# Moving one eighth of the output projection into the MLP pass, and splitting two sets of weights at other times, in a hand-scheduled attention + gMLP block

## The chip, the core and the metric

The kernel runs on one core of a Trainium2 chip. The metric is device time in microseconds (us) of the whole program, the median of several runs. Names used below: PE is TensorE (matmuls), ACT ScalarE, DVE VectorE, POOL GpSimd, SP the queue that issues most of the DMAs.

## The reference

One token block, S = 2048, D = 512, 32 heads of 16, F/2 = 896, all in float32:

```python
xn = layernorm(x)
q, k, v = heads(xn @ wqkv)                      # 32 heads of 16
o = softmax(q @ k.T * 16 ** -0.5) @ v
z = gelu(xn @ w_in)                             # 2048 x 1792
z1, z2 = z[:, :896], layernorm(z[:, 896:])
g = w_sp @ z2 + b_sp                            # 2048 x 2048 times 2048 x 896
out = x + heads_back(o) @ wo + (z1 * g) @ w_out
```

## The kernel before

**Precision.** A float32 operand is split into a rounded part and a remainder, [.., 0, ..] and [.., 1, ..] of one tile, and a product is three matmuls (high times high, low times high, high times low). The split of a weight tile is two POOL operations behind one load (`weight`, lines L286 and L288 for the function's two operations).

**Dense work.** All of the large projections go through `dense`: each *slot* is two matmuls that lie side by side in the upper and the lower 64 rows of the array, into the one PSUM tile `dps`. A *pass* (the two halves of `dps` filled and then read out) is 24 slots of z1 or z2, 96 of the spatial product, 42 of `mlp_out`, 24 of `attn_out`; the next pass can begin when `dps` has been copied out (`dfree`).

**Attention.** For each of 16 pairs of heads and 4 column groups, 16 key tiles: a score product *S* (then the exponential, on ACT, tile `pf`), a product *M* of the next pair whose row maximum DVE takes (tile `mm`, 128x1024), and in blocks of 8 key tiles a *value block V* of 32 matmuls (`sl<-pf,vall`). S, M and V share three PSUM tiles `sl`.

**The order.** A planner in the kernel walks through simulated time and writes the instructions of all engines in that order. Between two value blocks it goes through one line of `ORDER`, a string of S, M, D (one dense slot) and V. There are 128 value blocks, the last without M work behind it. The stretch behind block n is called *turn n* here, and turns 2k and 2k+1 together, from the start of block 2k to the start of block 2k+2, *pair k*: k runs from 1 to 63, and behind pair 63 stands block 128 and what is left. When no dense slot can be issued and nothing else either, PE gets a *filler* slot: two matmuls of zeros into `dps` (`filler`, `dps<-brow,zeror`). A slot list yields `"q"` at its ends: if more than 11 slots have gone into the turn, dense work holds until the next value block.

**Sequence of the dense work**, one generator after the other: `v_rest`, `qk_rest` (q and k of the other heads), `z2_all` (16 passes), `z1_all` (14 passes, gelu on POOL and ACT), `spatial` (w_sp times z2, 4 column groups of 512, each with 16 weight tiles `wsp`), `mlp_out` (7 blocks of `wout` against `hp`, the product z1 * g; the sum with x goes to a scratch), `attn_out` (4 blocks of `wo` against `op`, the normalised heads; the sum goes into `fin`, and `last_pair`, `last_mm`, `last_add` add the last pair of heads and store the result).

**Buffers.** Weights, z, and intermediate tiles live in one ring of 19 buffers (`piece`), counted by `room["big"]`; tasks start when `room` allows. `ahead_of_time` splits a weight tile early and writes both parts to a scratch in memory, from which `fetch_parts` reads them back; before the change the seven z1 weight tiles are handled so, right at the start. `norm_out(g4, c)` normalises eight heads of one column group (DVE, four POOL operations on `ob` and `ohl`, five DMAs) and writes them to `oscr`. It begins when its heads are done and the one buffer `ogrp` is free.

Of the kernel before, what the change touches and what calls it, by code (L numbers as in the profile page):

```python
# [16 lines left out]
P = 128  # L17
# [20 lines left out]
LEAD = 30  # L38
XAT = 8.0
# [17 lines left out]
def fused_block(ctx, tc, x, wqkv, wo, w_in, w_spT, b_sp, w_out, out):  # L57
# [56 lines left out]
    mscr = [dr.tile([4, 32, 32], F32, name=f"mscr{i}") for i in range(4)]  # L114
    w1scr = [dr.tile([P, 2, 512], F32, name=f"w1scr{f}") for f in range(NF)]
# [186 lines left out]
    def fetch_parts(out, k, scr, spare):  # L302
        yield "C", lambda: room["big"] > 1 + spare[0]
        t = piece(f"wf{k}")
        move(t, scr)
        yield "T", LOAD
        out[k] = t
# [314 lines left out]
    def z1_all():  # L622
        for g in range(NG):
# [52 lines left out]

    def load_b(g):
# [3 lines left out]
    def spatial():  # L681
        for n, (g, (x, y)) in enumerate(units):
            lone, opens, closes = x == y, x <= y, x >= y
            if n == 0:
                yield from need(lambda: room["t5"] > 3)
            if opens:
                for f in {x, y}:
                    load_z1(g, f)
# [11 lines left out]
            for s in range(NT):  # L700
# [14 lines left out]
                if s == 7:  # L715
                    yield "q",
            if lone:
# [49 lines left out]
    def mlp_load(t, q):  # L767
        hp = []
        for i, n in enumerate((4, 3)):
            h = piece(f"hp{t}_{q}_{i}")  # L770
            v = h[:, :, :n * P].rearrange("p a (f q) -> p a f q", q=P)
            for r, u in zip(HALVES, (t + q, t + 1 - q)):
                move(v[r], hscr[u // 4][r, :, u % 4, 4 * i:4 * i + n, :])
            hp.append(h)
        hps.append(hp)

    def mlp_out():
# [13 lines left out]
        for t in range(0, NT, 2):  # L791
            xt = load_x(t)
            if t == NT - 4:
                selectors()
                prepare(wo_, [(g, f"wo{g}", wo[g * P:(g + 1) * P, :], 512) for g in range(4)], spare=(-9,))
            for q in range(2):
# [7 lines left out]
                for f in range(NF):  # L804
# [3 lines left out]
                    yield from dense(1, ops, ops, (q, 1 - q), not q and f == 0, q == 1 and f == NF - 1)  # L808
# [4 lines left out]
        lease("big", NF)  # L813
# [49 lines left out]
    def norm_out(g4, c):  # L863
# [3 lines left out]
        yield open_("ogrp")  # L867
# [45 lines left out]
    def ao_load(t):  # L913
        ops = []
        for q in range(2):
            op = piece(f"op{t}_{q}").rearrange("p a (g q) -> p a g q", q=P)
            for r, u in zip(HALVES, (t + q, t + 1 - q)):
                for a in range(2):
                    move(op[r, a, 0:3, :], oscr[r, a, :, u * P:(u + 1) * P])
# [6 lines left out]
    def attn_out():  # L926
        def out_(t):
            yield "D", 1.22
# [4 lines left out]
        yield from need(lambda: len(wo_) == 4)  # L933
        for t in range(0, NT, 2):
# [5 lines left out]
            for q in range(2):  # L940
# [8 lines left out]
                yield from dense(4, lambda g: ops(g, False), lambda g: ops(g, True), (q, 1 - q), not q, q == 1)  # L949
# [54 lines left out]
    with tc.manual_schedule(engines=engines):  # L1004
# [325 lines left out]
```

## Time and profile before

| | |
|---|---|
| median of 3 runs | 1876.55 us (1875.42 to 1880.77) |
| the profiled execution | 1873.65 us, span 1871.9 us |
| granted PE clock | 0.994 |
| PE busy | 1821.7 us of matmuls, 1103.6 us of weight loads |
| DVE, ACT, POOL busy | 1443.5, 1188.7, 721.0 us |
| DMA | 297.75 MB, mean 159 GB/s |

Busy time of PE is a sum of windows that overlap in the pipeline, so 97% does not say that no matmul more would fit. What is of use here is the length of a pair (some 26 to 31 us) beside what stands in it.

### The profile page before, as it was taken

What the parts mean: (1) busy time and instruction counts of PE and PEld (TensorE: products, weight loads), DVE (VectorE), ACT (ScalarE), POOL (GpSimd) and SP (SyncE); (2) the same over time, 40 slices, a digit from 0 to 9 for tenths busy, and PEclk for the clock granted to TensorE, in tenths of its full rate; (3) what the DMA queues carried; (4) which work ended last, traced back from release to release, by engine and by line L of the source; (5) the groups of instructions that cost most, each with busy time, mean ns of one, the idle gap of its engine ahead of it and who ended that gap; (6) DMA issues with size and microseconds to landing.
All of it is one profiled execution on the core that took longest, in us unless ns stands there. A gap on an engine that the chain in (4) does not pass through costs nothing.

```text
span 1871.9 us, 38101 instructions
## 1 busy us (share of the span) xinstructions
PE 1821.7 (97%) x14848; PEld 1103.6 (59%) x14848; DVE 1443.5 (77%) x1677; ACT 1188.7 (64%) x1292; POOL 721.0 (39%) x808
## 2 busy tenths in 40 slices
PE   6989999999999999999999999999999999999998
PEld 5756566655654565466666656565655656555555
DVE  6568878888897887878787878777877878788863
ACT  2147777687676677766666666566656666666653
POOL 5412242778879768710145203400352222002110
PEclk9999999999999999999999999999999999999999
DMA  7836572533566343366568665744766757475544
GB/s 230 295 121 190 193 238 87 126 91 109 135 225 192 117 125 98 88 152 150 153 196 194 175 170 164 177 129 128 186 189 163 185 155 181 119 150 158 154 132 142
DMA packets 209309, 297.75 MB, mean 159 GB/s; under 512 B 36049, under 2 KB 107281, under 8 KB 206241
## 3 DMA queue, kind: packets, MB, share of 16 engines
q1 hardware_dynamic: 200008, 265.44, 51.8%
q0 software_dynamic: 9120, 29.89, 4.9%
q8 instruction: 116, 1.90, 0.4%
q14 instruction: 65, 0.52, 0.1%
HBM read 189.60 MB, written 105.65 MB: 158 GB/s over the span
## 4 chain that ended last, share of the span: by engine, by line
PE 85%; DVE 5%; POOL 4%; issue 2%; DMA 2%; ACT 1%; SPq 0%; DVEq 0%; POOLq 0%; ACTq 0%
PE dps L1181 33%; PE sl L1219 23%; PE sl L1122 14%; PE sl L1136 12%; DVE mm L839 4%; PE dps L1195 1%; POOL wsp L288 1%; ACT pf L74 1%; POOL wsp L286 1%; DMA zs<-z2scr 0%; PE sl L242 0%; PE sl L241 0%; PE sl L240 0%; POOL z2hl L542 0%; DMA kscr<-qkhl 0%
## 5 line engine op out<-in xcount | busy, mean ns | idle before, releaser
L839 DVE TENSOR_REDUCE mm<-sl 128x2 f32<-128x1024 f32 x1024 | 1224.2, 1222 | 209.2 <-PE sl L1136 204.7
L74 ACT ACTIVATE pf<-sl 128x1024 f32<-128x1024 f32 x1024 | 1041.1, 1026 | 337.3 <-PE sl L1122 300.1
L1219 PE MATMUL sl<-pf,vall 128*32 128x512 f32 x4096 | 467.3, 597 | 0.0
L1122 PE MATMUL sl<-qst,kst 50*128 50x512 f32 x2048 | 443.3, 422 | 14.0 <-DVE mm L839 5.1
L1181 PE MATMUL dps<-wsp,zs 64*128 64x512 f32 x2688 | 439.4, 393 | 2.7 <-DMA zs<-z2scr 2.7
L1136 PE MATMUL sl<-kst,qst 48*128 48x512 f32 x2048 | 427.1, 407 | 3.4 <-DVE mm L839 1.8
L1122 PEld LDWEIGHTS sl<-qst,kst 50*128 50x128 f32 x2048 | 197.7, 184 | 225.5 <-issue 84.0
L1181 PEld LDWEIGHTS dps<-wsp,zs 64*128 64x128 f32 x2688 | 265.0, 187 | 44.8 <-DMA zs<-z2scr 4.7
L1219 PEld LDWEIGHTS sl<-pf,vall 128*32 128x32 f32 x4096 | 120.3, 110 | 268.3 <-issue 236.1
L1136 PEld LDWEIGHTS sl<-kst,qst 48*128 48x128 f32 x2048 | 198.1, 185 | 109.6 <-ACT pf L74 57.6
L747 POOL TENSOR_TENSOR hhl<-z1i,hhl 128x512 fp32r<-128x512 f32 x28 | 35.6, 1284 | 371.4 <-ACT hhl L74 371.4
L74 ACT ACTIVATE e<-sl 128x512 f32<-128x512 f32 x64 | 38.2, 598 | 212.6 <-PE sl L1219 194.2
L1239 DVE TENSOR_TENSOR e<-sl,e 128x512 f32<-128x512 f32 x64 | 44.3, 692 | 132.3 <-PE sl L1219 68.9
L1181 PE MATMUL dps<-w,xt 64*128 64x448 f32 x768 | 110.8, 368 | 1.5
L1181 PE MATMUL dps<-wout,hp 64*128 64x512 f32 x672 | 109.6, 392 | 0.0
L882 POOL TENSOR_TENSOR ob<-ob 128x512 f32<-128x512 f32 (+1 forms) x16 | 20.5, 1282 | 193.6 <-DMA ob<-escr 193.6
L1181 PEld LDWEIGHTS dps<-w,xt 64*128 64x128 f32 x768 | 73.7, 186 | 16.1 <-issue 7.8
L438 POOL TENSOR_TENSOR qkhl<-qr,qkhl 128x512 fp32r<-128x512 f32 x24 | 30.4, 1283 | 129.5 <-ACT qkhl L74 93.3
L886 POOL TENSOR_TENSOR ob<-ob 128x512 f32<-128x512 f32 (+1 forms) x16 | 20.5, 1283 | 147.1 <-DMA ob<-rscr 147.1
L1181 PEld LDWEIGHTS dps<-wout,hp 64*128 64x128 f32 x672 | 65.2, 187 | 9.4
L1195 PE MATMUL dps<-brow,zeror 64*128 64x512 f32 x276 | 51.8, 399 | 0.5 <-DVE fin L929 0.3
L1181 PE MATMUL dps<-xnT,wqk 64*128 64x512 f32 x288 | 47.4, 396 | 1.1 <-ACT vall L74 0.4
(285 smaller groups left out, 1617.9 us busy)
## 6 DMA issues: line engine op xcount, KB each, us to landing
zs<-z2scr SPq DMA_DIRECT2D x192, 256.0 KB
escr<-e SPq DMA_DIRECT2D x60, 256.0 KB
hscr<-hhl POOLq DMA_DIRECT2D x28, 512.0 KB, 6.0
qst<-qscr SPq DMA_DIRECT2D x30, 384.0 KB
kst<-kscr SPq DMA_DIRECT2D x30, 384.0 KB
qscr<-qkhl SPq DMA_DIRECT2D x16, 512.0 KB
kscr<-qkhl SPq DMA_DIRECT2D x16, 512.0 KB
xscr<-xnT POOLq DMA_DIRECT2D x16, 512.0 KB, 6.7
```

The costliest lines, as they stand in the source:

```text
L74: return nc.scalar.activation(out, in_, func, **kw)
L438: nc.gpsimd.tensor_sub(hl[:, 1, :], raw_, hl[:, 0, :].bitcast(F32))
L747: nc.gpsimd.tensor_sub(hl[:, 1, :], z1, hl[:, 0, :].bitcast(F32))
L839: nc.vector.tensor_reduce(mmax[g][:, :, t, kc], sl[k], AX.X, ALU.max)
L882: nc.gpsimd.tensor_add(both_[rows, 0, :], both_[rows, 0, :], both_[rows, 1, :])
L886: nc.gpsimd.tensor_mul(both_[rows, 0, :], both_[rows, 0, :], both_[rows, 1, :])
L1122: nc.tensor.matmul(sl[k][:, j, :], kst[p % 2][rows, kt * P:(kt + 1) * P], qst[p % 2][rows, c * 512:(c + 1) * 512], start=True, stop=True)
L1136: nc.tensor.matmul(sl[k][:, j, :], qst[p % 2][rows, tt * P:(tt + 1) * P], kst[p % 2][rows, kc * 512:(kc + 1) * 512], start=True, stop=True)
L1181: nc.tensor.matmul(dps[:, bank, :w], lhs, rhs, start=go, stop=stop)
L1195: nc.tensor.matmul(dps[:, bank, :], zeror[r:r + 64], brow[r:r + 64], start=not begun, stop=not begun)
L1219: nc.tensor.matmul(sl[k][cols:cols + VW, 0, :], vpack(kt + r, 2 * p + j), pf[:, j * 512:(j + 1) * 512], start=n == n_pv, stop=n == n_pv + ...
L1239: nc.vector.tensor_add(e, sl[k][:, 0, :], e)
```

## The change

It has five parts:

- **An eighth block in `mlp_out`.** The rows of `wo` for heads 0 to 7 (`wo0`) are prepared with `wout`, and each pass of `mlp_out` takes an eighth block, the normalised first eight heads, loaded from `oscr` into the free quarter of the `hp` tile. `attn_out` takes 3 blocks in place of 4, so a pass of `mlp_out` has 48 slots in place of 42, and one of `attn_out` 18 in place of 24. Its read-out on DVE is issued only while a value block runs or after the last.
- **z1 weights later.** The `ahead_of_time` tasks of the seven z1 weight tiles are spawned at the start of `qk_rest`, not before the first scores.
- **Spatial weights earlier.** Eight of the 16 weight tiles of the first column group are split during `qk_rest` and written to a new scratch `wsscr`; they are fetched when z1 ends, and the other eight are split then.
- **`norm_out` of heads 0 to 7 waits** until eight quarters of the spatial product's input have been used (`OUTS`).
- The first `xnT` tiles of z1, and the first z1 tiles of the spatial product, are loaded by tasks of their own, and `z1_all` waits for the former, `spatial`'s read-out for the latter.

```diff
+KEPT = 8
+OUTS = 8
...
+    wsscr = [dr.tile([P, 2, 512], F32, name=f"wsscr{s}") for s in range(KEPT)]
...
     def qk_rest():
+        for f in range(NF):
+            owed[0] += 1
+            spawn(ahead_of_time(f, (f"w1_{f}", w_in[:, f * P:(f + 1) * P], D, ND), w1scr[f], AHEAD), 1)
         for g in (2, 3, 0, 1):
...
+                if (g, m) in ((3, 1), (0, 1)):
+                    for s in range(KEPT // 2) if g else range(KEPT // 2, KEPT):
+                        owed[0] += 1
+                        spawn(ahead_of_time(s, sp_weights(0, s), wsscr[s], AHEAD), 1)
...
+    fetched = [False]
+
+    def fetch_first():
+        for c in range(ND):
+            yield "C", lambda: room["big"] > 2
+            xnT[0, c] = piece(f"xnT0_{c}_")
+            move(xnT[0, c], xscr[0][c])
+        fetched[0] = True
+        late1[0] = 1
...
             if t == NT - 1:
-                yield from need(lambda: room["big"] > 5)
-                fetch_xnT(0)
-                late1[0] = 1
+                spawn(fetch_first(), 1)
...
     def z1_all():
+        yield from need(lambda: fetched[0])
...
-                    prepare(wsp, [((0, s), *sp_weights(0, s)) for s in range(NT)], spare=kept)
+                    for s in range(KEPT):
+                        spawn(fetch_parts(wsp, (0, s), wsscr[s], kept), 1)
+                    prepare(wsp, [((0, s), *sp_weights(0, s)) for s in range(KEPT, NT)], spare=kept)
...
-                    prepare(wout, [(f, f"wout{f}", w_out[f * P:(f + 1) * P, :], 512) for f in range(NF)], spare=(2,))
+                    prepare(wout, [(f, f"wout{f}", w_out[f * P:(f + 1) * P, :], 512) for f in range(NF)] + [(NF, "wo0", wo[0:P, :], 512)], spare=(2,))
...
             for r, u in zip(HALVES, (t + q, t + 1 - q)):
                 move(v[r], hscr[u // 4][r, :, u % 4, 4 * i:4 * i + n, :])
+                if i:
+                    move(h[r, :, n * P:], oscr[r, :, 0, u * P:(u + 1) * P])
...
-                for f in range(NF):
+                for f in range(NF + 1):
...
-        yield open_("ogrp")
+        yield "C", lambda: room["ogrp"] > 0 and (g4 or zused[0] > OUTS)
...
         def out_(t):
+            yield "C", lambda: mode == "V" or n_pv == N
             yield "D", 1.22
             nc.vector.tensor_add(fin[t], dps, fin[t])
...
-                yield from dense(4, lambda g: ops(g, False), lambda g: ops(g, True), (q, 1 - q), not q, q == 1)
+                yield from dense(3, lambda g: ops(g + 1, False), lambda g: ops(g + 1, True), (q, 1 - q), not q, q == 1)
...
-        for f in range(NF):
-            owed[0] += 1
-            spawn(ahead_of_time(f, (f"w1_{f}", w_in[:, f * P:(f + 1) * P], D, ND), w1scr[f], AHEAD), 1)
```

Where the instructions land shows in the order of the two programs. On SP, at the write of the first maxima (`mscr<-ms`) and their read back into the rows of q (`qst<-mscr`), on which the first scores wait, there stood before the loads of the z1 weights (`w_2r` to `w_5r`) and the writes of their parts (`w1scr`):

```order
L129 DMA w_2r<-in_w_in 128x4x128
L129 DMA w1scr_167<-w_0_885 128x1024
L129 DMA w1scr_168<-w_1_886 128x1024
L129 DMA w_3r<-in_w_in 128x4x128
L129 DMA w1scr_169<-w_2_908 128x1024
L129 DMA w_4r<-in_w_in 128x4x128
L129 DMA w_5r<-in_w_in 128x4x128
L129 DMA mscr_163<-ms_980 128x32
L129 DMA qst_90<-mscr_163 2x16x32 x2
```

and now:

```order
L132 DMA wqk_1r<-in_wqkv 128x4x128
L132 DMA mscr_163<-ms_966 128x32
L132 DMA qst_90<-mscr_163 2x16x32 x2
L132 DMA mscr_164<-ms_1167 128x32
L132 DMA qst_90<-mscr_164 2x16x32 x2
L132 DMA w_0r<-in_w_in 128x4x128
L132 DMA w_1r<-in_w_in 128x4x128
```

The seven loads and seven writes of the z1 weights now stand behind the first two of these round trips. On PE, in the first turn behind the last pass of z1, there stood before, between the S (`qst,kst`) and M (`kst,qst`) products, filler slots alone:

```order
L1122 MATMUL sl_195<-qst_91,kst_93 128x512 x2
L1136 MATMUL sl_193<-kst_92,qst_90 128x512 x2
L1195 MATMUL dps<-brow,zeror 128x512 x2
L1122 MATMUL sl_194<-qst_91,kst_93 128x512 x2
L1195 MATMUL dps<-brow,zeror 128x512 x4
L1136 MATMUL sl_195<-kst_92,qst_90 128x512 x2
```

and now, two turns earlier in the program, the spatial product with the fetched tiles (`wf`) against its input (`zs`):

```order
L1149 MATMUL sl_203<-qst_91,kst_93 128x512 x2
L1163 MATMUL sl_202<-kst_92,qst_90 128x512 x2
L1208 MATMUL dps<-brow,onesr 128x512 x2
L1208 MATMUL dps<-wf_0_7821,zs_7818 128x512 x6
L1149 MATMUL sl_201<-qst_91,kst_93 128x512 x2
L1208 MATMUL dps<-wf_0_7823,zs_7818 128x512 x2
```

The turns of zeros behind z1 are gone, and what follows stands earlier. At the end, on PE behind the last value block, where `on` and `e` belong to the last pair of heads, there stood before two passes of `attn_out` (this is the first half of them):

```order
L977 MATMUL sl_194<-sel,on_19811 128x512 x2
L977 MATMUL sl_195<-sel,on_19811 128x512 x2
L962 MATMUL sl_193<-e_3_19810,sel 32x128 x8
L1181 MATMUL dps<-wo_18600,op_0_19821 128x512 x6
L1181 MATMUL dps<-wo_18612,op_0_19821 128x512 x6
L1181 MATMUL dps<-wo_18633,op_0_19821 128x512 x6
L1181 MATMUL dps<-wo_18634,ohl_3_19688 128x512 x6
```

and now:

```order
L1007 MATMUL sl_201<-sel,on_19970 128x512 x2
L1007 MATMUL sl_203<-sel,on_19970 128x512 x2
L992 MATMUL sl_202<-e_3_19969,sel 32x128 x8
L1222 MATMUL dps<-brow,zeror 128x512 x16
L1007 MATMUL sl_201<-sel,on_20057 128x512 x2
L1007 MATMUL sl_203<-sel,on_20057 128x512 x2
```

No dense work is left behind the last value block.

More of the change, by code (lines that the diff above doesn't have):

```diff
@@ L303, in fetch_parts @@
         yield "C", lambda: room["big"] > 1 + spare[0]
-        t = piece(f"wf{k}")
+        t = piece(f"wf{len(out)}_{len(wsp)}")
         move(t, scr)
@@ L675, in load_z1, with first_z1 @@
         move(z1s[g, f], z1scr[f][:, g, :])
+    def first_z1(g, fs):
+        yield "C", lambda: room["t5"] > 3
+        for f in fs:
+            load_z1(g, f)
     def load_b(g):
@@ L683, in spatial @@
             lone, opens, closes = x == y, x <= y, x >= y
-            if n == 0:
-                yield from need(lambda: room["t5"] > 3)
             if opens:
-                for f in {x, y}:
-                    load_z1(g, f)
+                if n:
+                    for f in {x, y}:
+                        load_z1(g, f)
+                else:
+                    spawn(first_z1(g, (x, y)), 1)
                 yield "t", [[(0, 512, onesr[0:64], brow[0:64], True, False), *([] if lone else [(1, 512, onesr[64:128], brow[64:128], True, False)])]]
@@ L716, in spatial @@
                     yield "q",
+            yield from need(lambda: (g, x) in z1s and (g, y) in z1s)
             if lone:
@@ L807, in mlp_out @@
                     ops = lambda _: (h[:, 0, c], h[:, 1, c], wout[f][:, 0, :], wout[f][:, 1, :])
-                    yield from dense(1, ops, ops, (q, 1 - q), not q and f == 0, q == 1 and f == NF - 1)
+                    yield from dense(1, ops, ops, (q, 1 - q), not q and f == 0, q == 1 and f == NF)
                 lease("big", 2)
@@ L812, in mlp_out @@
                 yield "q",
-        lease("big", NF)
+        lease("big", NF + 1)
     stacks = [0]
@@ L931, in out_ @@
             added[t] = ends[0]
-        yield from need(lambda: len(wo_) == 4)
+        yield from need(lambda: len(wo_) == 3)
         for t in range(0, NT, 2):
```

4 lines of the change are left out of this document (2 added, 2 removed).

## The prediction

> **What bounds the kernel now.** I read the page first, then the span in stretches of one pair of turns each (PE's value blocks give the borders), then the time line at the stretches that fall out of line. The page:
>
> ```profile
> span 1871.9 us, 38101 instructions
> ...
> PE 1821.7 (97%) x14848; PEld 1103.6 (59%) x14848; DVE 1443.5 (77%) x1677; ACT 1188.7 (64%) x1292; POOL 721.0 (39%) x808
> ...
> L74 ACT ACTIVATE pf<-sl 128x1024 f32<-128x1024 f32 x1024 | 1041.1, 1026 | 337.3 <-PE sl L1122 300.1
> ```
>
> PE is never far from busy, but what would a slot less be worth? That the stretches tell: length, then busy time of PE, PEld, DVE, ACT and POOL with the count of instructions, granted clock, DMA share, GB/s.
>
> ```profile
> 353.95:382.23 28.28, 27.66 (x231) 17.13 (x229) 23.52 (x31) 20.02 (x23) 22.52 (x30) 1.00 0.39 114
> 520.00:547.00 27.00, 26.21 (x204) 14.02 (x203) 24.26 (x31) 17.50 (x18) 20.13 (x29) 1.00 0.68 215
> 574.55:605.12 30.57, 27.29 (x196) 13.88 (x195) 23.57 (x30) 19.00 (x22) 29.50 (x37) 0.93 0.63 176
> 605.12:633.47 28.35, 28.18 (x227) 16.34 (x225) 21.91 (x26) 19.05 (x22) 16.92 (x18) 0.95 0.25 86
> 687.80:714.95 27.15, 26.97 (x227) 16.50 (x225) 21.68 (x25) 19.92 (x23) 19.02 (x20) 1.00 0.15 54
> 742.09:768.22 26.13, 25.75 (x198) 13.25 (x196) 21.73 (x25) 19.25 (x22) 24.86 (x28) 1.00 0.48 132
> 768.22:794.15 25.93, 25.13 (x179) 10.81 (x177) 20.00 (x23) 18.02 (x20) 14.85 (x16) 1.00 0.09 32
> 794.15:820.74 26.59, 26.59 (x228) 16.22 (x226) 19.90 (x23) 16.85 (x17) 9.36 (x10) 1.00 0.70 167
> 980.54:1007.68 27.14, 27.12 (x227) 16.49 (x225) 21.94 (x25) 17.52 (x19) 23.01 (x24) 1.00 0.74 210
> 1007.68:1035.88 28.20, 28.09 (x236) 17.33 (x234) 20.61 (x25) 17.08 (x18) 1.29 (x1) 1.00 0.81 154
> 1169.50:1198.79 29.29, 28.29 (x232) 16.76 (x231) 22.51 (x25) 18.03 (x19) 19.15 (x20) 1.00 0.68 188
> 1359.78:1391.14 31.36, 29.64 (x233) 18.15 (x231) 22.91 (x27) 17.81 (x19) 21.02 (x22) 0.95 0.72 199
> 1711.90:1738.56 26.66, 26.29 (x219) 15.15 (x217) 22.66 (x26) 16.84 (x17) 8.56 (x9) 1.00 0.60 170
> 1765.21:1793.39 28.18, 27.73 (x243) 16.85 (x241) 23.80 (x29) 16.81 (x17) 4.13 (x4) 1.00 0.45 136
> 1793.39:1820.26 26.87, 26.46 (x230) 15.58 (x229) 15.63 (x22) 16.46 (x17) 1.27 (x1) 1.00 0.45 138
> 1820.26:1845.09 24.83, 24.66 (x218) 14.74 (x216) 6.80 (x8) 16.13 (x18) 4.12 (x4) 1.00 0.66 204
> 492.67:980.54 487.87, 480.40 (x3898) 277.89 (x3896) 392.10 (x448) 333.43 (x364) 279.18 (x313) 0.99 0.53 147
> ```
>
> The row at 768.22 is pair 24: no dense work, 24 fillers, 25.93 us. The next holds 49 slots of the spatial product and takes 26.59. The row at 1711.90 is an `mlp_out` pair with 42 slots and 2 fillers: 26.66, as long as a pair with 49. So a pair costs some 26 to 27 us whatever stands in it, up to 49 slots: each turn waits for its eight row maxima and exponentials as much as for PE. **What counts is how many pairs the dense work needs, and what is left when the 128 blocks are done.** Only the last three pairs, with few or no maxima, and the tail are paid in slots.
>
> **The change, by pairs.** The order of the two programs gives the slots of each pair (dense + filler); pairs 1 to 13 are alike:
>
> ```
> pair    14     15     16    17   18-21  22    23     24    59,60  61    62    63     behind block 128
> before  24+17  24+13  39+5  33   48     48    24+10  0+24  42+2   48    48    48     48+7
> after   48+1   24+13  48+2  48   48     49    23+11  49    36     18+7  36+1  18+11  0+15
> ```
>
> z1 begins in pair 15 in place of 16; the spatial product in the middle of pair 22 in place of 25; `mlp_out` in 51 in place of 53; `attn_out` in 59 in place of 61. From pair 30 on, the new program holds what the old one holds two pairs later.
>
> *Pairs 14 to 29.* Before, the same work took 18 pairs, 487.87 us. Now 16: pair 14 is a full z2 pair, 28.3 (as the row at 353.95); pair 15 as the row at 520.00, 27.0; 16 and 17 full z1 pairs, 27.5 each; 18 to 22 five times 27.15 (row 687.80), 135.8; 23 as the row at 742.09, 26.1; 24 to 29 six times 26.65, 159.9. Sum 432.1, less by 55.8.
>
> *The borders between column groups.* Before, the first costs 27.14 + 28.20 against 2 x 26.6, so 2.1; the second 29.29, 2.7; the third 31.36, 4.8, where PE waits for `zs`:
>
> ```profile
> 1383.70 0.49 PE L1181 MATMUL dps<-wsp,zs 64*128 64x512 f32 x1 [1.22 <-DMA zs<-z2scr]
> 1384.69 0.50 PE L1181 MATMUL dps<-wsp,zs 64*128 64x512 f32 x1 [0.50 <-DMA zs<-z2scr]
> 1386.40 1.04 PE L1122 MATMUL sl<-qst,kst 50*128 50x512 f32 x2
> ```
>
> That load stands on SP behind the last raw weight tile, which waits for POOL's splits. Normalising a group of heads (`ob`) stood between those splits at the first and third border; since the borders move by two pairs and the heads do not, it now stands only at the first, and there twice. In the order the first two borders now show the form of the old first, the third that of the old second: 2.1 + 2.1 + 2.7 against 9.6, less by 2.7; I take 2.
>
> *`mlp_out`, eight pairs.* 48 slots and a filler, 26.65 by the spatial rows, against 26.66. DVE's read-out is the same. I take +0.1 each, +0.8. The eighth block's load is a 64-row piece behind the `hp` loads on SP, hidden a turn ahead; `wo0` is the last of eight splits on POOL before pair 51, and PE would wait there for one split if it came late. Heads 8 to 15 wait for the `ogrp` buffer that heads 0 to 7 now hold later, but nobody reads them before pair 59.
>
> *Pairs 59 and 60* are new: 36 slots and no filler, between 25.93 and 28.3; 27.0 each (more on that below), +54.0. The read-out of `attn_out`, now issued only beside a value block, stands behind the row maxima on DVE; `dps` stays full until then, and dense work holds until that block in any case.
>
> So pair 61 begins at 1765.21 - 55.8 - 2 + 0.8 + 54.0, 3.0 us earlier.
>
> *The end.* One slot is 0.23 us, one value block 3.57, by these steps of the chain (8 matmuls are 4 slots):
>
> ```profile
> 76.34 0.92 PE dps L1181 x8
> ...
> 119.27 3.57 PE sl L1219 x32
> ```
>
> Pair 61 drops from 48 to 25 slots, 5.4 us of PE, but cannot go under some 26: 27.0, less by 1.2. Pair 62 (six M left) drops by 11 slots, 2.6 us; I take 2.1, since ACT needs 16 exponentials. Pair 63 drops by 19 slots, 4.4 us; 16 exponentials of 1.03 us and the wait around two value blocks set a floor near 22, so 2.5. Behind block 128 the two passes go:
>
> ```profile
> 1849.91 2.35 DVE L984 TENSOR_TENSOR fin<-sl,fin 128x1024 f32<-128x1024 f32 x2 [0.34 <-PE sl L977]
> 1853.17 0.29 DVE L970 TENSOR_TENSOR on<-sl,on 128x128 f32<-128x128 f32 x1
> 1863.84 1.14 PE L977 MATMUL sl<-sel,on 32*128 32x512 f32 x8
> 1865.09 2.35 DVE L984 TENSOR_TENSOR fin<-sl,fin 128x1024 f32<-128x1024 f32 x2
> ```
>
> The last product (L977) needs `on`, ready at 1853.46, and two free `sl`, which the DVE operation at 1849.91 gives back before that. Now nothing stands ahead of it: 1853.55, 10.3 us earlier, and the last addition and store follow with it. The end gives 1.2 + 2.1 + 2.5 + 10.3 = 16.1.
>
> *The start.* At the first scores (the rows of stretches first):
>
> ```profile
> 90.00:100.00 10.00, 9.20 (x78) 6.99 (x76) 9.19 (x13) 1.08 (x2) 5.65 (x7) 1.00 1.02 393
> 100.00:110.00 10.00, 7.35 (x42) 4.83 (x38) 3.90 (x4) 3.09 (x3) 5.24 (x7) 0.83 0.63 206
> ...
> 162.78:189.85 27.07, 26.90 (x227) 16.38 (x225) 21.78 (x25) 20.09 (x23) 5.03 (x4) 1.00 0.64 223
> ...
> 97.92 0.69 SPq L129 DMA_DIRECT2D mscr<-ms  x1
> 102.91 1.41 SPq L129 DMA_DIRECT2D qst<-mscr  x2
> 119.00 0.32 SPq L129 DMA_DIRECT2D mscr<-ms  x1
> 121.78 1.28 SPq L129 DMA_DIRECT2D qst<-mscr  x2
> ...
> 105.20 0.99 PE L1122 MATMUL sl<-qst,kst 50*128 50x512 f32 x2 [2.56 <-DMA qst<-mscr]
> ```
>
> The first `mscr` write takes 4.99 us until its reader goes out, among z1 weights at 393 GB/s; the second 2.78. With the weights gone, PE waits 2.2 us less. Behind the wait the clock falls: a mean of 0.83 over 10 us is 3.4 us at half clock, 1.7 us of work lost. I take 3.9. The bounds are 4.3 (the whole wait goes) and, if the `xscr` writes are what fills the DMAs, 0. The splits move into pairs 1 to 5, where POOL is busy 5.03 us of 27.07; their writes stand on SP before `xnT` fetches and the next heads' `qst`, and a split that came late would hold those back: -1 at the worst, as long as SP is a pair ahead.
>
> *Does POOL keep up in pairs 14 to 17?* z1's gelu is five POOL operations per half pass; the order now asks for two more passes by the end of pair 17, four gelus, 4 x 4.76 = 19.0 (20 operations, 19.02, in the row at 687.80). What `norm_out` took there goes:
>
> ```profile
> 492.67:605.12 112.45, 13.42 (x12) 0.98 0.63 188
> 492.67:605.12 112.45, 107.02 (x824) 58.12 (x823) 93.62 (x117) 76.44 (x84) 98.07 (x123) 0.98 0.63 188
> ```
>
> (first `ob` alone, then all.) 98.07 - 13.42 + 19.0 = 103.7 us of POOL in the 110.3 that I gave the four pairs. That is tight, and where it failed before (574.55, ACT stuck behind a tanh that waited for POOL) it cost 30.57 - 27.15 and 1.2 in the pair behind: 4.6. I put down 2.1 of that.
>
> **Half clock.** The rows at 1384.69 and 1386.40 show half clock behind stops of 1.22 and 0.50 us. Pairs 59 to 63 end each turn with S and M alone and no filler, PE used to about a third for 3 us, in one turn (123) for 8; I put half of it into the 27.0 above. [...]
>
> **Sum.** 3.0 + 16.1 + 3.9 - 2.1 = 20.9 us less than the profiled execution's 1873.65, so 1852.75. The median shown lies 2.9 above that execution: **1855.6**.
>
> **Rivals.**
> - *POOL does not keep up* (0.16): if it is busy 87% of the time at best, as in 98.07 of 112.45, 103.7 us need 119 and not 110.3, so 8.7 - 2.1 more: 1862. For it: the row at 574.55. Against: the normalisation that leaves.
> - *The start gains nothing* (0.09), the DMA traffic being that of others: 1859.5.
> - *The change does not do what it says* (0.08): work pulled ahead makes its pairs longer by as much, and only 22 fillers go (276 matmuls become 232), 22 x 0.23 = 5.1: 1871.4. Against it: 25.93 beside 26.59.
> - *Slower: the clock* (0.05). If the thin turns 118 to 127 bring half clock that lasts through their value blocks, each 3.57 us longer, ten blocks cost 35 us and the end 1889. It decides from 2.1 us per turn. Against it: clock 1.00 in the rows at 742.09 and 768.22, though with fillers that the new turns lack. [...]
>
> The forecast has 0.62. A measurement of this kernel can tell about 0.3%, 5.6 us. Faster by more: 0.62 + 0.16 + 0.09 + half of the third, 0.91; within: 0.04; slower: 0.05. The range: down to 1848 (start 4.3, no POOL loss, 26 for pairs 59 to 61, borders 2.7, the last three pairs at their full slots), up to 1867 (the two first rivals together, and half clock at some of the ten turns).
>
> **What would show it.** Right: block 1 some 4 us earlier; z1 pairs from pair 16 on at 27 to 28; the 16 pairs from 14 on take 432; the borders cost 7; `out` stores 16 us behind block 128's start. Wrong: a pair above 29 between 14 and 17; clock below 0.9 in pairs 59 to 63; pairs with 49 slots in `mlp_out` at 28.

## The result, and the profile after

The changed kernel takes 1863.13 us (median of 6 runs, 1861.57 to 1869.64) beside 1875.3 us before (6 runs): a ratio of 0.9938, 95% interval 0.9919 to 0.9957. It is faster by 11.5 us in span and by 12.2 in the medians, where 20.9 were forecast: the direction was right, and somewhat over half of the gain came.

The page of the changed kernel:

```profile
span 1860.4 us, 38081 instructions
...
PE 1811.4 (97%) x14804; PEld 1099.5 (59%) x14804; DVE 1441.5 (77%) x1677; ACT 1189.1 (64%) x1292; POOL 722.3 (39%) x808
```

Busy time of PE says little again (10.3 us less). The stretches say where the time is; the columns are those of the prediction's rows:

```profile
186.62:214.73 28.11, 27.23 (x226) 16.77 (x224) 21.80 (x25) 20.12 (x23) 9.57 (x10) 1.00 0.69 248
490.49:924.96 434.47, 429.93 (x3555) 254.62 (x3553) 347.88 (x398) 300.67 (x330) 250.22 (x282) 1.00 0.57 160
924.96:1494.98 570.02, 566.82 (x4761) 345.09 (x4759) 448.34 (x505) 364.88 (x378) 178.81 (x182) 1.00 0.66 175
1140.34:1172.35 32.01, 30.19 (x236) 18.37 (x235) 20.77 (x25) 16.97 (x18) 3.15 (x3) 0.95 0.64 145
1494.98:1711.37 216.39, 215.10 (x1813) 132.67 (x1811) 172.39 (x188) 135.64 (x137) 23.00 (x27) 1.00 0.64 156
1711.37:1765.20 53.83, 51.73 (x402) 28.09 (x401) 46.33 (x53) 33.54 (x34) 6.71 (x6) 1.00 0.40 121
1765.20:1793.50 28.30, 26.46 (x197) 12.46 (x195) 22.19 (x26) 16.85 (x17) 5.42 (x5) 0.97 0.18 51
1793.50:1822.23 28.73, 27.15 (x208) 14.25 (x206) 15.52 (x21) 16.20 (x18) 4.12 (x4) 0.91 0.38 119
1822.23:1844.27 22.04, 20.75 (x180) 10.80 (x178) 6.75 (x7) 14.82 (x17) 0.00 (x0) 1.00 0.13 48
1844.27:1860.40 16.13, 10.29 (x96) 4.59 (x94) 6.56 (x7) 1.78 (x2) 0.00 (x0) 0.98 0.35 131
```

The second row is pairs 14 to 29: 434.47 us, against 487.87 for the 18 pairs before. The two new pairs 59 and 60 (1711.37) take 53.83, pair 63 (1822.23) 22.04, and what is left behind block 128 16.13 in place of 26.81. These are the forecast's sizes. Four stretches are longer than forecast: pair 3 (28.11; 27.04 before), pair 38 at the second border (32.01), the `mlp_out` pairs (216.39, 27.05 each), and pairs 61 and 62 (28.30 and 28.73, where 27.0 and 24.8 were expected). Where PE waits in pair 38, and what happens at the end of pair 61, the time line shows (start, length, engine, line; in brackets the idle time ahead and its releaser):

```profile
1152.62 0.50 PE L1208 MATMUL dps<-wsp,zs 64*128 64x512 f32 x1 [1.26 <-DMA zs<-z2scr]
1153.51 1.22 PE L1208 MATMUL dps<-wsp,zs 64*128 64x512 f32 x3 [0.38 <-DMA zs<-z2scr]
1154.10 1.05 PE L1149 MATMUL sl<-qst,kst 50*128 50x512 f32 x2
...
1788.03 0.49 PE L1149 MATMUL sl<-qst,kst 50*128 50x512 f32 x2 [0.63 <-DVE mm L868]
1789.16 0.50 PE L1149 MATMUL sl<-qst,kst 50*128 50x512 f32 x2 [0.32 <-DVE mm L868]
1791.59 0.80 PE L1149 MATMUL sl<-qst,kst 50*128 50x512 f32 x2 [0.30 <-DVE mm L868]
1793.50 6.05 PE L1246 MATMUL sl<-pf,vall 128*32 128x512 f32 x32
```

In pair 38 a late `zs` stops PE for 1.64 us, and the score product behind it takes 1.05 us in place of some 0.5 (the clock is 0.50 from 1153.28 to 1156.69 us). In turn 123 there is no dense work and no filler from 1786.9 on; PE serves S and M alone with stops of 0.63, 0.32 and 0.30 us, the product at 1791.59 takes 0.80 us in place of 0.50, and block 124 takes 6.05 us where a value block takes 3.6 (the clock is 0.50 from 1791.57 to 1798.40 us).

### The profile page after: what moved, and what is told of

It reads as the page before. It is cut to its first block, busy times and chain, and to the rows that moved or that the text cites. A ratio compares the mean times of both kernels' runs of the same rounds, so it can differ in the third digit from the quotient of the medians.

```text
span 1860.4 us, 38081 instructions
## 1 busy us (share of the span) xinstructions
PE 1811.4 (97%) x14804; PEld 1099.5 (59%) x14804; DVE 1441.5 (77%) x1677; ACT 1189.1 (64%) x1292; POOL 722.3 (39%) x808
## 4 chain that ended last, share of the span: by engine, by line
PE 84%; DVE 6%; DMA 4%; POOL 3%; issue 2%; ACT 1%; SPq 1%; DVEq 0%; POOLq 0%; ACTq 0%
PE dps L1208 34%; PE sl L1246 23%; PE sl L1149 13%; PE sl L1163 12%; DVE mm L868 4%; PE dps L1222 1%; DMA zs<-z2scr 1%; DMA kscr<-qkhl 1%; SPq L132 1%; ACT pf L76 1%; POOL wsp L291 1%; DMA wsp_15r<-in_w_spT 0%; POOL wsp L289 0%; DMA wsp_0r<-in_w_spT 0%; DMA qst<-mscr 0%
## 5 line engine op out<-in xcount | busy, mean ns | idle before, releaser
L1149 PE MATMUL sl<-qst,kst 50*128 50x512 f32 x2048 | 437.8, 419 | 11.1 <-DVE mm L868 4.3
L1208 PE MATMUL dps<-wsp,zs 64*128 64x512 f32 x2352 | 382.1, 393 | 2.6 <-DMA zs<-z2scr 2.6
L1208 PEld LDWEIGHTS dps<-wsp,zs 64*128 64x128 f32 x2352 | 229.3, 187 | 40.4 <-DMA zs<-z2scr 4.1
L1208 PE MATMUL dps<-wout,hp 64*128 64x512 f32 x672 | 110.3, 392 | 0.0
L1208 PE MATMUL dps<-wf,zs 64*128 64x512 f32 x336 | 55.5, 392 | 0.1
```

Of the source, the lines that this page charges most:

```text
L1149: nc.tensor.matmul(sl[k][:, j, :], kst[p % 2][rows, kt * P:(kt + 1) * P], qst[p % 2][rows, c * 512:(c + 1) * 512], start=True, stop=True)
L1208: nc.tensor.matmul(dps[:, bank, :w], lhs, rhs, start=go, stop=stop)
```

## The experiments

The theory to test: the account by pairs holds, and most of what is missing is lost to late data (pairs 3 and 38) and to half clock behind turn 123 (pair 62). The main rivals: the eighth block or the early split is itself what gains, and the long pairs at the end are as long as their row maxima on DVE. Each kernel is compared with before on the same chip; the changed kernel itself was run again beside three of them only, so the other differences from it go by two ratios and are known to some 3 us. Profiles of the same instructions differ by up to 2 us in the start alone (block 1 begins at 113.9 to 116.0 in the kernels that share the changed kernel's start), so pairs are compared where a single profile is used.

**Without the eighth block.**

```diff
-                for f in range(NF + 1):
+                for f in range(NF):
...
-                yield from dense(3, lambda g: ops(g + 1, False), lambda g: ops(g + 1, True), (q, 1 - q), not q, q == 1)
+                yield from dense(4, lambda g: ops(g, False), lambda g: ops(g, True), (q, 1 - q), not q, q == 1)
```

> The changed kernel with seven blocks in the MLP pass and four in the output projection again; everything else stays. Theory (a pair of turns costs 26 to 27 us whatever stands in it, and what counts is only what is left behind value block 128; in the order nothing dense is left there in this kernel either): the eight MLP pairs fall from 27.05 to 26.66 (-3.1 in all), pairs 59 to 63 take 27 + 27 + 28.2 + 26.2 + 22.5 = 130.9 against the changed kernel's 132.9, the tail stays 16.1; 5 us less than the changed kernel, a span of 1855. Rival (the eighth block is what shortens the end, priced by slots as in the prediction): pairs 61 to 63 grow by 1.2 + 1.2 + 0.2 and the MLP pairs fall by 0.1 each, so about 2 us more than the changed kernel, 1862.

1859.88 us, ratio 0.9924 (0.9911 to 0.9937); span 1858.6. Pairs 51 to 58 and pairs 59 to 63 in its stretches:

```profile
1490.90:1704.73 213.83, 210.71 (x1730) 122.49 (x1729) 171.81 (x188) 135.16 (x137) 22.86 (x27) 1.00 0.59 148
1704.73:1842.54 137.81, 132.74 (x1062) 73.18 (x1060) 90.55 (x105) 82.56 (x85) 16.22 (x15) 0.96 0.34 105
```

The `mlp_out` pairs fall by 2.6 us, as both expectations had it in sign; the end is 5 us longer than the changed kernel's 132.9 and not 2 shorter, half clock again among it (0.96): value blocks 122 and 127 take 4.76 and 6.34 us of the chain in place of 3.57, which is 4.0 of the 5. By these pairs the eighth block gains some 2.4 us, less than this half clock alone; the medians do not show it (the two intervals overlap, and the seven-block kernel has the lower middle). What the block is worth by itself stays open; it is not where the 12 us come from.

**The start alone, in the kernel before.**

```diff
     def qk_rest():
+        for f in range(NF):
+            owed[0] += 1
+            spawn(ahead_of_time(f, (f"w1_{f}", w_in[:, f * P:(f + 1) * P], D, ND), w1scr[f], AHEAD), 1)
```

(and the same lines taken out ahead of the first scores)

> The kernel before with one edit: the splits of the z1 weights are spawned at the start of qk_rest and not ahead of the first scores. Theory of the prediction: pair 1 begins 3.2 to 3.9 us earlier than before, as in the changed kernel, but a part is given back in pair 3 (28.11 against 27.04 in the changed kernel), so 2.2 us are left at pair 14 and at the end: 1871.9 - 2.2 = 1869.7 of span. Rival (the earlier start of the changed kernel is not due to the weights but to run-to-run spread, or all of it is given back): 1871 to 1873.

1870.14 us, 0.9978 (0.9969 to 0.9987), so 4.1 us by the medians. Pair 3, and pairs 17 and 18:

```profile
184.63:211.66 27.03, 26.86 (x226) 16.27 (x224) 21.69 (x25) 20.08 (x23) 5.04 (x4) 1.00 0.44 158
570.04:600.87 30.83, 27.72 (x196) 14.06 (x194) 23.86 (x30) 19.09 (x22) 29.68 (x38) 0.91 0.65 177
600.87:630.33 29.46, 29.28 (x226) 16.85 (x225) 21.64 (x26) 19.00 (x22) 16.70 (x17) 0.92 0.24 83
```

The start is worth what the prediction said (3.9) by the medians; in this one profile block 1 begins at 113.91 in place of 119.20 us, 5.3 earlier, of which 3.7 are left in the span. Nothing is given back in pair 3: there the DMA share is 0.44, in the changed kernel 0.69. So it is not the z1 weights alone that cost the changed kernel a us in pair 3. The jam of POOL at pair 17 stands as before.

**No early split of the spatial weights.**

```diff
-KEPT = 8
+KEPT = 0
```

> The changed kernel with KEPT = 0: no spatial weight is split ahead, all 16 tiles of the first column group are split when z1 ends. In the order the spatial product then runs one turn later from pair 24 on, and nothing dense is left behind value block 128 all the same. Theory (the count of turns is 128 either way, so a turn of delay costs nothing as long as the tail stays empty; only what is late inside a turn costs): pairs 23 to 25 cost 1 us more, the second border (32.01 us in the changed kernel, where the rows of the order read 25/19 and 27/26 slots) reads 24/25 and 24/24 here and falls to 27, the third from 29.2 to 28, pairs 59 to 63 stay within 2 us of 132.9: span 1853 to 1857. Rival (the early split is what gains, a turn of dense work being worth its 13 us): 1860.4 + 13 = 1873.

1867.73 us, 0.996 (0.9948 to 0.9972), 4 to 5 us more than the changed kernel. Pairs 23 to 25, and pair 38:

```profile
736.30:762.48 26.18, 25.45 (x192) 12.24 (x190) 19.51 (x23) 17.09 (x20) 15.27 (x16) 1.00 0.19 61
762.48:790.14 27.66, 27.34 (x214) 15.16 (x212) 20.54 (x23) 17.44 (x18) 7.56 (x8) 1.00 0.70 169
790.14:819.25 29.11, 28.50 (x236) 17.02 (x235) 21.79 (x25) 17.48 (x20) 0.74 (x1) 1.00 0.46 121
...
1143.44:1176.17 32.73, 29.63 (x228) 18.45 (x226) 20.24 (x23) 17.01 (x17) 11.61 (x14) 0.95 0.59 149
```

Between the two expectations: a turn of delay does not cost its 13 us, since pairs 59 to 63 take 133.5 with all the dense work a turn later and the tail still empty. What it costs are pairs 23 to 25 (82.95 in place of 79.49) and the borders, which do not get shorter as I had read from the order: pair 37 takes 29.09, pair 38 32.73. So the order's slot counts of these two turns did not foretell the length of the border.

**Without the wait of the read-out.**

```diff
         def out_(t):
-            yield "C", lambda: mode == "V" or n_pv == N
             yield "D", 1.22
```

> The changed kernel without the wait that puts the read-out of the output projection beside a value block: dps comes free earlier in the turn, and zeros fill what is left of it. In the order pairs 59 to 63 hold 36+8, 36+8, 36+3, 17+16 and 19+6 slots (dense + filler). Theory (pair 62 took 28.73 us because turn 123 ran on S and M alone, the clock halved, and block 124 took 6.05 us in place of 3.64): the clock is 1.00 in pairs 59 to 63, no value block is above 4 us, pairs 61 and 62 take 27 and 25.5; 4 us less, span 1856. Rival (these pairs are as long as their maxima on DVE, to which the read-outs in mid-turn are added, 2.35 us for two): pairs 59 to 61 grow to 28 to 29 and 62 stays at 28; span 1861 to 1865.

1865.43 us, 0.995 (0.9938 to 0.9962), 2 to 3 us more than the changed kernel, with intervals that overlap. Pairs 59 to 62:

```profile
1709.08:1737.79 28.71, 27.95 (x219) 15.34 (x217) 23.87 (x28) 16.80 (x18) 5.39 (x5) 1.00 0.42 132
1737.79:1766.50 28.71, 27.94 (x218) 15.56 (x216) 22.91 (x27) 16.73 (x18) 1.27 (x1) 1.00 0.30 90
1766.50:1795.81 29.31, 27.14 (x224) 14.99 (x222) 22.62 (x26) 16.73 (x17) 5.41 (x5) 1.00 0.30 91
1795.81:1822.31 26.50, 24.08 (x200) 12.60 (x198) 14.15 (x20) 16.74 (x18) 4.12 (x4) 1.00 0.28 89
```

Both were half right. Clock 1.00 in the four, no value block above 4 us, pair 62 at 26.50: the clock stayed full in this profile. That the zeros kept it is not shown, since turn 123 has no zeros here but a whole pass of 18 slots; the zeros stand in turn 124. Pairs 59 and 60 take 1.8 us more each, as the rival had it, pair 63 takes 24.25 in place of 22.04 (why, is not shown), and that is more than the clock was worth: pairs 59 to 63 take 137.5 in place of 132.9. By these pairs the wait earns its place. The run does not separate the read-outs in mid-turn from the 8 filler slots that it adds to each of the two pairs, which at 0.23 us a slot are 1.8 us of PE as well; that the read-outs are the cause is argued.

**The changed kernel again,** beside the next three.

> The changed kernel once more, unaltered, as the neighbour of the next kernels. Its first profile began value block 1 at 115.96 us where four kernels with the same start began it at 113.9 to 114.0; the granted clock there was 0.91 between 40 and 60 us. If that was chance, block 1 begins at 114 and the span is 1858.4; the second border (pair 38) 30 to 32, the pairs 61 and 62 again 28.3 and 28.7. If the start belongs to the kernel, 116 and 1860.4.

1862.37 us, 0.9934 (0.992 to 0.9948). Block 1 at 115.27; pair 38, pairs 61 and 62:

```profile
1140.43:1169.73 29.30, 28.71 (x237) 17.39 (x235) 20.66 (x25) 17.00 (x18) 2.10 (x2) 1.00 0.66 149
1762.56:1791.04 28.48, 26.83 (x197) 12.57 (x195) 22.44 (x26) 16.86 (x17) 5.41 (x5) 0.94 0.19 57
1791.04:1819.15 28.11, 26.55 (x209) 14.30 (x207) 15.40 (x21) 16.19 (x18) 4.14 (x4) 0.94 0.38 122
```

The start differs by chance, within 2 us. So does the second border: in the seven profiles of kernels with the same work there pair 38 took 29.20, 29.30, 29.84, 32.01, 32.01, 32.30 and 33.07 us. Pairs 61 and 62 are long again, with half clock.

**A buffer for the last heads.** The fifth pass of `attn_out` begins only when the last heads of its column group are normalised (`lasthl`), and their normalisation waits for the one `ogrp` buffer. So the pass begins late in turn 122 and ends early in turn 123, and the rest of that turn has no dense work.

```diff
-        yield "C", lambda: room["ogrp"] > 0 and (g4 or zused[0] > OUTS)
-        lease("ogrp", -1)
+        ring = g4 == 3 and c >= 2
+        yield "C", lambda: room["big"] > 1 if ring else room["ogrp"] > 0 and (g4 or zused[0] > OUTS)
+        lease("ogrp", 0 if ring else -1)
...
-        both_ = at_.tile([P, 2, 512], F32, tag="ogrp", name=f"ob{g4}_{c}", bufs=1)
+        both_ = piece(f"ob{g4}_{c}").bitcast(F32) if ring else at_.tile([P, 2, 512], F32, tag="ogrp", name=f"ob{g4}_{c}", bufs=1)
```

> The changed kernel, but the normalisation of the last heads takes a ring buffer of its own for column groups 2 and 3 and does not wait for the one that group 1 holds. In the order each of the turns 118 to 125 then has one whole pass of 18 slots; turn 123 is not left to S and M. Theory (pairs 61 and 62 are long because the wait for that one buffer empties turn 123, the clock halves there and block 124 runs at half clock): pair 61 27.0, pair 62 26.0, pair 63 (23 fillers, no slot) 22, no value block above 4 us: 4 us less than the changed kernel. Rival (they are long because of their row maxima and exponentials, whatever PE does): 61 and 62 stay above 28 and 27.5, 1 us less at the most.

1857.13 us, 0.9909 (0.9894 to 0.9924), 5.2 less than the changed kernel beside it by the medians. Pairs 59 to 63 account for 2.1 to 2.7 of that (130.24 us, beside 132.38 and 132.90 in the two profiles of the changed kernel); the rest is not traced. Pairs 61 to 63:

```profile
1763.60:1791.69 28.09, 26.79 (x218) 14.54 (x216) 23.49 (x27) 16.80 (x17) 4.11 (x4) 1.00 0.34 100
1791.69:1817.64 25.95, 24.45 (x206) 13.38 (x204) 16.10 (x20) 15.61 (x17) 0.00 (x0) 1.00 0.19 65
1817.64:1839.63 21.99, 20.23 (x166) 9.18 (x166) 4.62 (x6) 15.58 (x18) 0.00 (x0) 1.00 0.13 48
```

Pair 62 is what the theory said, 25.95, with the same 36 slots that took 28.1 to 28.7 at a clock of 0.91 to 0.94. Pair 61 is what the rival said: 28.09 with 36 slots, 28.30 with 18, 28.18 with 48 before. Between 18 and 48 it does not go by slots. The long half is turn 123, 14.2 to 14.4 us in these profiles where turn 121 takes 12.9 to 13.3 us; in it DVE has two operations on `on` (0.96 and 0.28 us) beside its eight or nine maxima, and stands idle for 1.2 to 3.1 us ahead of them. No run moves these two operations, so that they set the length is argued.

**Spread slots.** In addition, every fourth place for a dense slot is passed over while `attn_out` runs.

```diff
+        def thin(op):
+            return len(queue) == 1 and n_pv < N and ORDER[line][:at_op + 1].count("D") % 4 == 0
...
-            gone = {"S": n_st == N, "M": n_mx == NSTEP, "D": ahead > 0 or not has_dense(t), "V": n_pv == N}[op]
+            gone = {"S": n_st == N, "M": n_mx == NSTEP, "D": ahead > 0 or thin(op) or not has_dense(t), "V": n_pv == N}[op]
```

> As the kernel with the buffer of its own, and in the output projection every fourth place for a dense slot is passed over, so that its 18 slots reach to the end of the turn and leave no stretch of S and M alone. If these stretches cost anything by themselves, pairs 59 to 62 fall from 26.9 to 26.2 each, 2 to 3 us in all; if a turn is as long as its eight maxima and exponentials, nothing changes, within 0.5 us over the five pairs.

1857.02 us, 0.9903 (0.9887 to 0.9919). Pairs 59 and 60 take 26.69 and 26.64 in place of 27.14 and 27.07, pairs 61 and 62 28.04 and 25.64: 1.2 us less over the four, between the two expectations, and below what the medians can tell. Its profile has the dearest pair 3 of all, where PE waits 2.6 us for `qst` and the clock is 0.95 in the mean:

```profile
185.72:217.06 31.34, 28.60 (x227) 19.00 (x225) 21.83 (x25) 20.27 (x23) 9.93 (x11) 0.95 0.67 244
```

**Heads 8 to 15 behind the second border.**

```diff
-        yield "C", lambda: room["ogrp"] > 0 and (g4 or zused[0] > OUTS)
+        yield "C", lambda: room["ogrp"] > 0 and (g4 or zused[0] > OUTS) and (g4 != 1 or c < 3 or zused[0] > 68)
```

> The changed kernel, but the normalisation of heads 8 to 15 of the last column group waits until the second border is past (block 80 in place of 75). Theory (it loads 0.54 MB among the weight tiles and the zs loads of that border, where the DMA engines are 0.9 busy for some 25 us, and so holds zs back): the zs wait of 1.6 us and the half clock behind it go, pair 38 falls from 32.0 (29.8 to 32.3 in three runs of the same instructions) to 28.5. Rival (the 1.5 MB of the next pair of heads' q and k, and the buffers that PE gives back late, hold zs back): pair 38 stays at 30 to 32.

1859.47 us, 0.9918 (0.9905 to 0.9932), 2.9 less than the changed kernel beside it, in four runs within 1.3 us. Pair 38:

```profile
1140.10:1168.32 28.22, 28.04 (x236) 17.55 (x235) 20.20 (x23) 16.98 (x18) 0.00 (x0) 1.00 0.57 133
```

28.22, and 28.22 and 28.24 in the two kernels below that have the edit too, where the seven without it spread from 29.20 to 33.07. In its profile PE does not wait for `zs` there. The normalisation beside that border is what makes `zs` late. The loads of q and k are still there, so they alone are not enough.

**The three edits together, and the eight splits one by one.** The second kernel of the two has this in addition:

```diff
+        early = [ahead_of_time(s, sp_weights(0, s), wsscr[s], AHEAD) for s in range(KEPT)]
         for g in (2, 3, 0, 1):
...
-                if (g, m) in ((3, 1), (0, 1)):
-                    for s in range(KEPT // 2) if g else range(KEPT // 2, KEPT):
-                        owed[0] += 1
-                        spawn(ahead_of_time(s, sp_weights(0, s), wsscr[s], AHEAD), 1)
+                if g != 2 and early:
+                    owed[0] += 1
+                    spawn(early.pop(0), 1)
```

> The changed kernel with three edits at once: the last heads' normalisation has a buffer of its own, the output projection's slots are spread over the turn, and heads 8 to 15 of the last column group are normalised behind the second border. If the gains are independent (5.2 us and 2.9 us in the medians of the two kernels that had them alone, the spread worth 1 us in pairs 59 and 60), the median is 8 to 9 us under the changed kernel's, near 1854, pair 38 at 28.2, pair 62 at 25.7. If they overlap (both let the same late runs go), 5 us, 1857.

> As the three edits together, and the eight spatial weight tiles are split one at each step of q and k from the fourth on, not four at a time. Pair 3 took 28.1 to 31.3 us in the kernels that split four there, and 27.0 in the two that split none, with the read of the maxima's rows issued 5 us later on SP and the DMA engines 0.96 busy in pair 2. Theory (the burst of loads and writes holds that read back): pair 3 at 27.1, the others within 0.2, so 1 to 2 us less than the three edits together and fewer high runs. Rival (the z1 weights, which stay where they are, hold it back, or the splits now disturb pairs 4 to 8 instead): no difference in the sum of pairs 2 to 8.

The three together: 1856.06 us, 0.9903 (0.989 to 0.9917). With the splits one by one: **1853.9 us, 0.9892 (0.9879 to 0.9906)**, in four runs from 1852.84 to 1855.28: the best of all, 20.4 us less than before on the same chip. Pairs 3 and 62 of the one, then of the other:

```profile
184.67:212.99 28.32, 27.17 (x227) 16.82 (x225) 21.80 (x25) 20.24 (x23) 9.32 (x10) 1.00 0.70 250
1787.91:1815.10 27.19, 26.10 (x206) 13.81 (x205) 15.36 (x20) 15.60 (x17) 0.00 (x0) 0.94 0.19 63
```

```profile
185.80:212.87 27.07, 26.90 (x226) 16.47 (x224) 21.71 (x25) 20.10 (x23) 8.86 (x8) 1.00 0.69 241
1787.31:1812.95 25.64, 24.56 (x206) 13.56 (x205) 15.31 (x20) 15.59 (x17) 0.00 (x0) 1.00 0.20 66
```

Pair 3 falls to 27.07 and the pairs behind it do not grow: pairs 2 to 8 take 192.53 us with the three edits and 190.93 here. The burst of four splits was what held back the read of the row maxima (`qst<-mscr`): counted from block 1, it goes out on SP after 68.9 us in the changed kernel, after 66.1 here and after 65.6 without the early split. The three edits together gain less than the sum of their parts, and in their profile pair 62 is one reason: half clock came back there, with the same instructions that kept the full clock in the other. The two medians differ by 2.2 us, with intervals that overlap; the profiles by 1.25 us in pair 3 and 1.55 in pair 62.

**Heads 0 to 7 at their old place.**

```diff
-OUTS = 8
+OUTS = -1
```

> The changed kernel without the wait of heads 0 to 7 (OUTS = -1): they are normalised in turns 26 to 35 again, as before the change. The prediction held that POOL just keeps up in pairs 14 to 17 because this work is gone from there. Theory: with it POOL would need 98.07 + 19.0 = 117 us in the 112.3 of these four pairs, pair 17 gets long and loses 24 slots (in the order it holds 4+20), the four pairs take 116 to 118 in place of 112.3 and the spatial product begins most of a turn later; 4 to 6 us more than the changed kernel, 1867. Rival (POOL has more reserve than that, and the second border, now without any normalisation beside it, falls to 28): 3 us less than the changed kernel.

1867.92 us, 0.9965 (0.9952 to 0.9979). Pairs 14 to 17 in one, then 16 and 17:

```profile
490.07:608.40 118.33, 112.28 (x840) 62.77 (x838) 93.28 (x118) 78.39 (x88) 107.15 (x133) 0.94 0.64 187
546.30:577.96 31.66, 29.35 (x227) 17.88 (x227) 22.17 (x28) 17.70 (x19) 30.03 (x36) 0.95 0.79 217
577.96:608.40 30.44, 28.53 (x180) 13.93 (x178) 22.21 (x28) 20.16 (x24) 26.15 (x33) 0.83 0.46 132
```

118.33 in place of 112.3, and 5 us more than the changed kernel, as the theory had it. POOL is busy 107.15 of 118.33 us, and the delay of these heads is what makes room for the early z1. Not all of the 6 us is POOL's directly, as the rows show half clock too (0.83 in pair 17). The first border pays now: pair 31 takes 32.03, pair 38 27.51.

**No zeros in pair 23.**

```diff
-            elif t - active > 0.15 and dfree[0] <= t and len(begun) != 1 and not swap:
+            elif t - active > 0.15 and dfree[0] <= t and len(begun) != 1 and not swap and not 8 * 45 <= n_pv < 8 * 48:
```

> The changed kernel without the 11 slots of zeros in pair 23 (turns 46 and 47, which hold 12 and 10 slots of the spatial product); nothing else is left out and the output is the reference's. Theory (a few us of S and M alone are enough to halve the clock): clock 0.9 or below in pair 23, a value block of 5 to 7 us at its end, pairs 23 and 24 together 2 to 4 us longer than 52.8. [...]

1864.93 us in a single run. Pairs 23 and 24, and the end of turn 46:

```profile
738.32:764.26 25.94, 23.99 (x174) 11.12 (x172) 20.66 (x23) 17.77 (x20) 15.74 (x17) 1.00 0.44 133
764.26:791.42 27.16, 27.05 (x231) 16.88 (x229) 19.99 (x23) 16.79 (x17) 0.00 (x0) 1.00 0.76 151
```

```profile
747.79 0.50 PE L1149 MATMUL sl<-qst,kst 50*128 50x512 f32 x2 [0.24 <-DVE mm L868]
751.30 0.50 PE L1163 MATMUL sl<-kst,qst 48*128 48x512 f32 x2 [0.24 <-DVE mm L868]
751.76 3.64 PE L1246 MATMUL sl<-pf,vall 128*32 128x512 f32 x32
```

Clock 1.00 and 53.10 us beside 52.82: in this one profile the theory did not hold. Some 5 us of S and M alone, with stops of up to 0.24 us, did not halve the clock ahead of the value block at 751.76, which takes 3.64 us; a longer stretch in turn 123 (6.7 to 7.2 us), with a stop of 0.60 to 0.63, did so in all four profiles that have it (0.91 to 0.94 in the mean of pair 62). That the zeros are for nothing does not follow from one execution; the last section says why.

## Why the prediction was right, and where its sizes were off

Right by its own steps, with some luck where it is said:

- *Two pairs fewer for the same work.* Pairs 14 to 29 take 434.47 us; the 432.1 and the POOL reserve of 2.1 make 434.2. POOL keeps up, and the run with heads 0 to 7 at their old place shows that their delay is what lets it. But there was luck in it: pairs 14 to 17 take 112.28, the 110.3 and the reserve, with POOL busy 98.79 us and not the 103.7 of the sum, so POOL had to be busy for 88% of the time, hardly more than the rival's 87%. (With heads 0 to 7 at their old place it reaches 91%, so 87% is no limit.) Pair 16 took 28.96 in one profile and 29.04 in the other, at the edge of the sign named for being wrong.
- *The start,* 3.9: 3.2 in the changed kernel's first profile, 3.9 in its second, 4.1 in the medians of the start alone. Block 1 of the other kernels with this start lies 3.3 to 5.3 us earlier than in the one profile before, so the bound of 4.3 was too narrow for single profiles.
- *Pairs 59 and 60* at 27.0 (26.94 and 26.89). This is luck in part: 0.6 us of each 27.0 was my estimate for half clock, which no run shows there: their clock was 1.00, and with the slots spread over the turn they take 26.69 and 26.64.
- *Pair 63* at 22.3 (22.04), the *tail* 10.3 us shorter (10.68).
- *The rival of lasting half clock in ten turns* did not come: in its two profiles one value block of the ten was slow.

Off in size, 9.4 us in the first profile:

- *The last three pairs* (5.0 longer; the tail gives 0.4 back). The term for pair 61 was priced by slots with a floor of 26; it takes 28.0 to 28.5 with 18, 36 or 48 slots. What sets it is not shown; the two `on` operations on DVE are a candidate. Pair 62 was put at 24.8; it takes 25.6 to 25.95 at full clock, and the half clock out of turn 123 adds 2 to 3 us. I had put half of that stretch into pairs 59 to 61, where next to nothing of it is paid, and none into 62, where block 124 stands.
- *The `mlp_out` pairs* (2.0 above the +0.8). 48 slots take 27.05, not 26.75 (27.88 in the first of the eight, 26.93 in the mean of the others). With passes that begin one turn later (the kernel with heads 0 to 7 at their old place) the seven pairs 52 to 58 take 26.67 each; why the turn matters is open.
- *The start* (1.7): 0.7 of it in the first profile's start, 1.0 in pair 3. The prediction named that mechanism, a split that holds back what stands behind it on SP, for the z1 weights alone, and gave it 1 at the worst. It came with the four spatial weights, which had no term, and cost 0.5 to 4.3.
- *The borders* (1.0 over pairs 30 to 50). The second was to cost 2.1 and cost 5.9 in the first profile (3.1 to 6.9 in the seven), against the same 2 x 26.6. I followed the normalisation of heads 0 to 7 to the first border. That heads 8 to 15 wait behind them for the one buffer I saw, and took for harmless since nobody reads them before pair 59; they land on the second border.

Two small sums are off: 23 slots at 0.23 are 5.3 us and not 5.4, and 35 us on top of 1855.6 are 1890.6 and not 1889. Nothing rests on either.

On half clock the runs are less plain than I took them to be. It stood behind stops of 1.26 and 0.38 us in pair 38, and of 0.63, 0.32 and 0.30 us ahead of block 124; but the zeros of pair 23, which I took to be needed, were not in the one profile without them (1.00). The same instructions had half clock in pair 62 in one kernel (0.94) and not in another (1.00).

## What to carry to other kernels

Where a count of turns is fixed, moving work ahead is worth only what it takes off the end and off the turns that stall; the early split of eight weights, one of the larger edits, was worth 4 to 5 us and not the turn that it saved. When one user of a single buffer is delayed, follow the whole queue behind it: both misses that could be mended (the second border, the empty turn 123) were later users of the buffer that the change had held back. Spread background transfers one by one: four at once cost 0.5 to 4.3 us at a read that the critical engine waits for, one at a time nothing in the one profile.

## What the runs showed of the hardware that I had not expected

Whether half clock came was partly a matter of chance in these runs. Ahead of value block 125 the kernel with three edits and the one with the splits one by one have the same instructions and the same stops, to 0.01 us; the first:

```profile
1800.72 0.50 PE L1164 MATMUL sl<-kst,qst 48*128 48x512 f32 x2 [0.20 <-ACT pf L76]
1801.46 0.74 PE L1150 MATMUL sl<-qst,kst 50*128 50x512 f32 x4 [0.23 <-DVE mm L868]
1802.62 5.17 PE L1247 MATMUL sl<-pf,vall 128*32 128x512 f32 x32 [0.42 <-DVE mm L868]
```

and the second:

```profile
1800.12 0.51 PE L1164 MATMUL sl<-kst,qst 48*128 48x512 f32 x2 [0.21 <-ACT pf L76]
1800.84 0.74 PE L1150 MATMUL sl<-qst,kst 50*128 50x512 f32 x4 [0.22 <-DVE mm L868]
1802.02 3.64 PE L1247 MATMUL sl<-pf,vall 128*32 128x512 f32 x32 [0.43 <-DVE mm L868]
```

5.17 us and 3.64 us, in a pair 62 whose clock is 0.94 in the one and 1.00 in the other. The clock records of two profiles, of the changed kernel and of the one before, have seven stretches at half clock between 30 us and the last ones, which reach the end. They begin at 40.53, 1153.28 and 1791.57 us after the change and at 34.31, 105.99, 600.92 and 1385.99 before it; those at 600.92 and 1791.57 last 6.83 us, the others 3.41. Within each profile the distances between their starts are whole multiples of 3.4133 us, to 0.02 us (326 and 187 of them in the changed kernel). In the 3.41 us ahead of the four that begin behind 110 us, 10 to 12 matmuls began. But in the kernel without zeros 12 began in the 3.41 us from 747.79 on, and the clock of pair 23 stayed 1.00, so their number alone does not decide. That it matters how a thin stretch falls on these starts is my estimate from the distances; no run tests it.

A thin stretch has to be priced as a chance, not as a cost or as nothing; and the span of one profile of this kernel is uncertain by some 3 us (an estimate from the pairs above) for this and the two late transfers, so single edits of 2 us were read from their pairs.
